# Attention's weight-value products written contiguously, eight of the 128 on VectorE

## The chip, the core and the metric

The kernel runs on one NeuronCore of a Trainium2 chip. The metric is the device time of one execution in microseconds (us). The core has five engines that run side by side: PE (TensorE, matmul; its weight loads are listed apart as PEld), DVE (VectorE), ACT (ScalarE), POOL (GpSimd) and SP, which here only issues DMAs. Each engine executes its own instructions in order and waits for other engines on semaphores. SBUF is the working memory of 128 partitions, PSUM holds what PE writes.

## What is computed

A block over 2048 tokens of width 576: the input plus a sliding, dilated attention plus a dense layer with mish, both fed with the layer-normed input.

```python
def _A_ref(x, wqkv, wo):
    H = 32; Dh = D // H                      # 18
    W, dil = 8, 2
    qkv = (x @ wqkv) split into q, k, v of 32 heads
    idx = pos[:, None] - (arange(W) * dil)[None, :]
    logits = einsum("bhsd,bhswd->bhsw", q, k[idx]) * scale   # -1e9 where idx < 0
    attn = softmax(logits)
    o = einsum("bhsw,bhswd->bhsd", attn, v[idx])
    return o @ wo
def _B_ref(x, w1, b1, w2):
    h = x @ w1 + b1                          # 4608 wide
    return (h * tanh(softplus(h))) @ w2
xn = layernorm(x)
return x + _A_ref(xn, wqkv, wo) + _B_ref(xn, w1, b1, w2)
```

Each token attends to 8 earlier tokens, two apart. The change concerns the line with `o`: 8 weights times 8 value vectors of 18 numbers, summed over the 8.

## The kernel before

The tokens are taken in two halves of 1024. Matmuls are made from fp32 numbers that are split into a rounded part and a remainder, so most operands exist twice, and ACT, DVE and POOL spend much of their time making those splits. PE runs the projections of q, k and v (L360, in the second half partly L478), the first dense layer (L706, L712) and the second dense layer (L809 in the first half, L898 in the second), then the output projection (L1028). Results of the second dense layer are added up by DVE from PSUM into SBUF: L813 in the first half, L904 in the second. They use the four PSUM banks of the tag `out`; each group of six matmuls fills one bank, and PE can write a bank again once DVE has read it. L751 on DVE adds up parts of the first dense layer from the four banks of the tag `h`.

The attention isn't done on PE. It is a generator, `attention(hf)`, one for each half, that works through 8 pairs of units, a unit being two heads (36 numbers). Token position is laid out as 128 partitions x 8 tokens (`TJ`). For each pair:

- scores: for each of the two units `k` and each half `c` of the tokens, POOL multiplies q with a window of k (L583, two instructions of 576 elements, output `pr`), and DVE sums over the 18 numbers of a head (L588);
- softmax: DVE takes maxima, sums and reciprocals (L602 to L614), ACT the exponential (L608);
- weights times values: for each unit `k` and head `h`, POOL multiplies the weights `L` with a window of v (L621, two instructions of 576 elements, output `pv`), and DVE sums over the 8 window positions into `og` (L627).

The products `pr` and `pv` share two buffers. The sum of one step (`red`) is held back by one step: `flush()` at the start of the next step issues it. The steps of the generator are spread over the program by a plan with due times, in which everything is placed at numbered positions among PE's items; the resulting order on each engine is fixed. So where an instruction stands is set by the code's order alone, and an engine that waits at one of them holds up all that stand behind it on that engine.

In L619 to L627 `pv` is laid out token, number, window position. The sum over the window then reads 8 neighbouring floats, and the multiply, which runs token, window position, number, writes with a step of 8 floats.

Of the kernel before, what the change touches and what calls it, by code (L numbers as in the profile page):

```python
# [8 lines left out]
F32 = mybir.dt.float32  # L9
F32R = mybir.dt.float32r  # L10
AF = mybir.ActivationFunctionType
ALU = mybir.AluOpType
AX = mybir.AxisListType.X

S, D, F = 2048, 576, 4608
H, DH, W, DIL = 32, 18, 8, 2
HALO = (W - 1) * DIL
P = 128
# [4 lines left out]
TJ = SH // P  # L23
# [6 lines left out]
PU = 2  # L30
# [14 lines left out]
def block_kernel(ctx: ExitStack, tc: tile.TileContext, x, wq, wo, w1, b1, w2, mask, out):  # L45
    nc = tc.nc
# [8 lines left out]
    sb = ctx.enter_context(tc.tile_pool(name="sb", bufs=2))  # L55
# [87 lines left out]
    def newton1():  # L143
        newton(rs1, ve1, y1, nc.gpsimd)
        nc.gpsimd.tensor_mul(nm1, mv1[:, :, 0:1], rs1)
        nc.gpsimd.tensor_scalar(nm1, nm1, -1.0, None, op0=ALU.mult)
# [372 lines left out]
    def load_kv(hf, i, part):  # L519
        g, u = divmod(i, UQ)  # L520
        t = odd.tile([P, TJ + HALO, CU], F32, tag="kv", bufs=4, name=f"kv{part}_{hf}_{i}")
        src = kv_d[g][part * UQ + u, hf * SH, 0:1]
        nc.sync.dma_start(
            t.rearrange("p t c -> p (t c)"),
            bass.AP(tensor=src.tensor, offset=src.offset, ap=[[TJ * CU, P], [1, (TJ + HALO) * CU]]))
        return t

    def load_kq(hf, i):
        g, u = divmod(i, UQ)
        k = load_kv(hf, i, 0)  # L530
        q = odd.tile([P, TJ, CU], F32, tag="q", bufs=2, name=f"q_{hf}_{i}")
        nc.sync.dma_start(q, q_d[g][u, hf * SH:(hf + 1) * SH, :]
                          .rearrange("(p j) c -> p j c", j=TJ))
        return k, q

    def win(kv, c0, cn, j0, jn):
        base = kv[:, j0, c0:c0 + 1]
        return bass.AP(tensor=base.tensor, offset=base.offset,
                       ap=[list(base.ap[0]), [CU, jn], [DIL * CU, W], [1, cn]])
# [10 lines left out]
    def soon(slots, phase, fn, *key):  # L550
        i = now[0] // U + slots
        if phase == 3 and i == at["m", 0, 1, 0]:
            phase = 5
        put(i * U + phase, fn, " ".join(str(x) for x in key))
# [6 lines left out]
    def attention(hf):  # L561
        kqs = [load_kq(hf, k) for k in range(PU)]
        yield
        behind = [None]

        def flush():
            if behind[0] is not None:
                behind[0]()
                behind[0] = None

        for pair in range(NQ * UQ // PU):
            n = f"{hf}_{pair}"
            vs, nxt = [], []
            L = sb.tile([P, PU, TJ, W, 2], F32, tag="L", bufs=2, name=f"L_{n}")
            hj = TJ // 2
            for k, (kt, q) in enumerate(kqs):
                for c in range(2):
                    flush()
                    pr = sb.tile([P, hj, W, CU], F32, tag="pr", bufs=2, name=f"pr_{n}_{k}_{c}")
                    j0 = c * hj  # L580
                    hh = hj // 2
                    for x in range(0, hj, hh):
                        nc.gpsimd.tensor_tensor(  # L583
                            out=pr[:, x:x + hh], in0=q[:, j0 + x:j0 + x + hh, None, :].to_broadcast([P, hh, W, CU]),
                            in1=win(kt, 0, CU, j0 + x, hh), op=ALU.mult)

                    def red(pr=pr, k=k, j0=j0, L=L):
                        nc.vector.tensor_reduce(  # L588
                            L[:, k, j0:j0 + hj].rearrange("p j w h -> p (j w h)"),
                            pr.rearrange("p j w (h d) -> p (j w h) d", h=2), axis=AX, op=ALU.add)  # L590
                    behind[0] = red
                    if k == 0:
                        vs.append(load_kv(hf, pair * PU + c, 1))
                    yield
            flush()
            if hf == 0:
                lm = L[0:2].rearrange("p k j w h -> p k (j w h)")
                nc.vector.tensor_add(lm, lm, mk[:, None, :].to_broadcast([2, PU, TJ * W * 2]))
            m = odd.tile([P, PU * TJ, 2], F32, tag="m", bufs=2, name=f"m_{n}")
            Lf = L.rearrange("p k j w h -> p (k j) w h")  # L600
            Lt = Lf.rearrange("p j w h -> p j h w")
            nc.vector.tensor_reduce(m, Lt, axis=AX, op=ALU.max)  # L602
            mb = m[:, :, None, :].to_broadcast([P, PU * TJ, W, 2])
            nc.vector.tensor_sub(Lf, Lf, mb)
            Ls = L.rearrange("p k j w h -> p (k j w h)")
            if (hf, pair) == (0, 4):
                soon(1, 0, lambda: nc.scalar.preload_act_table_set("natural_log_exp_and_others"), "exp", n)
            soon(1, 0, lambda Ls=Ls: nc.scalar.activation(Ls, Ls, AF.Exp, scale=SCALE), "exp", n)  # L608
            if (hf, pair) == (0, 4):
                soon(1, 0, root1, "exp", n)  # L610
            yield
            nc.vector.tensor_reduce(m, Lt, axis=AX, op=ALU.add)
            nc.vector.reciprocal(m, m)
            nc.vector.tensor_mul(Lf, Lf, mb)  # L614
            og = sb.tile([P, TJ, PU * CU], F32, tag="og", bufs=1, name=f"og_{n}")
            for k, vt in enumerate(vs):
                for h in range(2):
                    flush()
                    pr = sb.tile([P, TJ, DH, W], F32, tag="pr", bufs=2, name=f"pv_{n}_{k}_{h}")  # L619
                    for x in range(0, TJ, hj):  # L620
                        nc.gpsimd.tensor_tensor(  # L621
                            out=pr[:, x:x + hj].rearrange("p j d w -> p j w d"),
                            in0=L[:, k, x:x + hj, :, h:h + 1].to_broadcast([P, hj, W, DH]),
                            in1=win(vt, h * DH, DH, x, hj), op=ALU.mult)

                    def red(pr=pr, og=og, c0=k * CU + h * DH, last=(k, h) == (PU - 1, 1), pair=pair):
                        nc.vector.tensor_reduce(og[:, :, c0:c0 + DH], pr, axis=AX, op=ALU.add)  # L627
                        if last:
                            nc.sync.dma_start(
                                o_d[hf][:, pair * PU * CU:(pair + 1) * PU * CU]  # L630
                                .rearrange("(p j) c -> p j c", j=TJ), og)
                    behind[0] = red
                    if (hf, pair, k, h) == (0, *(4, 0, 1)):
                        newton1()
                    if k == 0 and (pair + 1) * PU + h < NQ * UQ:
                        nxt.append(load_kq(hf, (pair + 1) * PU + h))
                    yield
            kqs = nxt
        flush()
        yield  # L640
# [661 lines left out]
    def spot(hf, q, i):  # L1302
        return at["s", hf, q, i]
# [48 lines left out]
    for m, lists in ((0, DIFFS), (1, DIFFS), ("w", DIFFS), ("w", SPLITS)):  # L1352
        for n, steps in enumerate(lists):
            for st_ in steps.split():
                f = dict(l=d_load, s=d_sum, h=d_high, o=d_low, k=d_keep)[st_[0]]
# [43 lines left out]
    for n in range(8):  # L1399
        c, k = divmod(n, 4)  # L1400
        d = i + (0, 1, 3, 5, 7, 9, 11, 13)[n]
        before(d, lambda c=c, k=k: s_step(1, c, k))
        d = max(d + 2, (at["q", 1, 1, 1, 2], at[("z", 1, 2)])[c] if k == 3 else 0)
# [47 lines left out]
    for i in range(len(plan)):  # L1451
        w = [r_ for m, r_ in zip(marks, rate) if m <= i][-1:] or [0]
# [4 lines left out]
    k = marks[0] - 1  # L1457
    for n in range(2 * steps):
        t = n * total / (2 * steps)
        if n == steps:  # L1460
            k = max(k, spot(1, 0, 0) + 1)
        k = next(k for k in range(k + 1, len(plan)) if T[k + 1] > t and ok[k])
        hf = n // steps
        if n % steps == 0:
            before(k - 4, lambda hf=hf: (att.__setitem__(hf, attention(hf)), next(att[hf])), f"first {hf}")
        before(k, lambda hf=hf: next(att[hf], None), f"att {n}", 2)
        cuts.append(k)
# [5 lines left out]
    j = items[7 * (OC - 1) + 2][2]  # L1473
# [64 lines left out]
```

## Time and profile before

| | us |
|---|---|
| median of 3 runs | 1105.64 |
| lowest, highest | 1104.11, 1105.72 |
| the profiled execution: time | 1108.94 |
| the profiled execution: first to last instruction | 1106.8 |

The granted TensorE clock of the profiled execution is 0.997 on the mean. A row of a group names the source line, the engine, the operation, output<-inputs, the shapes and the count, then the busy time in us and the mean of one in ns, and behind the bar the idle time of the engine just before them with what ended it. A row of the timeline has the start and the length in us, then the same names; `x4` merges four neighbours, and the idle time before stands in brackets. Ends of PE's rows are modelled, so that a row may run a little into the next.

### The profile page before, as it was taken

How to read it: one execution, taken by the hardware profiler on the slowest of the kernel's cores; microseconds unless marked ns; L12 is line 12 of the kernel's file. 1: busy time of each engine (PE TensorE's matmuls, PEld its weight loads, DVE VectorE, ACT ScalarE, POOL GpSimd, SP SyncE). 2: the span in 40 equal slices, each digit the busy share in tenths (PEclk: the TensorE clock that was granted, in tenths of full speed). 3: DMA queues.
4: the chain of work that ended last, by engine and by line, in shares of the span. 5: the costliest groups of instructions: out<-in, count | busy, mean ns of one | idle time of the engine just before them, and what ended most of it. 6: DMA issues, size and time to landing. Idle time of an engine off the chain costs nothing.

```text
span 1106.8 us, 18262 instructions
## 1 busy us (share of the span) xinstructions
PE 1096.2 (99%) x6510; PEld 1009.7 (91%) x6510; DVE 862.5 (78%) x1425; ACT 516.4 (47%) x943; POOL 837.1 (76%) x675
## 2 busy tenths in 40 slices
PE   9999999999999999999999998999999999999998
PEld 8999989999999999999999887999999999999998
DVE  6447699999898888888746467788888768789876
ACT  5543646446456455546333253534444443444332
POOL 2598787897678676888799658787697978678852
PEclk9999999999999999999999998999999999999999
DMA  6789897889789698888799696665666665675863
GB/s 237 247 282 304 270 329 251 307 318 339 282 272 323 246 326 308 307 314 278 251 296 325 174 335 244 238 241 213 211 215 249 242 249 193 237 257 177 290 207 104
DMA packets 166909, 290.23 MB, mean 262 GB/s; under 512 B 31234, under 2 KB 106532, under 8 KB 166820
## 3 DMA queue, kind: packets, MB, share of 16 engines
q1 hardware_dynamic: 166820, 289.08, 75.9%
q8 instruction: 51, 0.84, 0.3%
q14 instruction: 38, 0.31, 0.1%
HBM read 170.71 MB, written 118.32 MB: 261 GB/s over the span
## 4 chain that ended last, share of the span: by engine, by line
PE 96%; DVE 1%; DMA 1%; issue 1%; ACT 0%; DVEq 0%
PE h L706 31%; PE po L809 20%; PE po L898 18%; PE pq L360 11%; PE h L712 6%; PE o L1028 5%; PE z L478 3%; DMA z_B<-kept_wq 1%; PE ta L86 0%; PE ot L942 0%; PE ot L958 0%; DMA acc<-in_x 0%; DVE st L123 0%; PE ot L960 0%; DVE accP L904 0%
## 5 line engine op out<-in xcount | busy, mean ns | idle before, releaser
L809 PEld LDWEIGHTS po<-w,act 128*128 128x128 f32 x1728 | 236.4, 188 | 6.3 <-DVE acc L813 0.4
L809 PE MATMUL po<-w,act 128*128 128x288 f32 x1728 | 240.9, 295 | 0.0
L898 PEld LDWEIGHTS po<-pw,u 128*128 128x128 f32 x1512 | 206.6, 188 | 4.7
L898 PE MATMUL po<-pw,u 128*128 128x288 f32 x1512 | 209.6, 295 | 0.0
L583 POOL TENSOR_TENSOR pr<-q,kv 128x576 f32<-128x576 f32 x128 | 192.1, 1527 | 12.3 <-DVE og L627 8.6
L621 POOL TENSOR_TENSOR pv<-L,kv 128x576 f32<-128x576 f32 x128 | 176.4, 1480 | 27.3 <-ACT rt L740 16.0
L813 DVE TENSOR_TENSOR acc<-po,acc 128x288 f32<-128x288 f32 x288 | 118.7, 448 | 32.9 <-PE po L809 31.7
L360 PE MATMUL pq<-wq,xt 128*128 128x432 f32 x672 | 136.2, 361 | 1.3 <-ACT xt L92 1.1
L904 DVE TENSOR_TENSOR accP<-po,accP 128x288 f32<-128x288 f32 x240 | 101.2, 450 | 41.2 <-PE po L898 40.2
L360 PEld LDWEIGHTS pq<-wq,xt 128*128 128x128 f32 x672 | 125.1, 188 | 8.2 <-ACT xt L92 1.7
L706 PE MATMUL h<-xt,t 128*128 128x512 f32 x432 | 111.6, 394 | 0.3 <-DVE c L751 0.3
L706 PE MATMUL h<-S,t 128*128 128x512 f32 x432 | 110.3, 391 | 0.0
L706 PE MATMUL h<-xt,wa 128*128 128x512 f32 x432 | 105.8, 394 | 2.8 <-DVE rm L751 2.8
L706 PEld LDWEIGHTS h<-xt,wa 128*128 128x128 f32 x432 | 81.7, 190 | 20.7 <-DVE rm L751 3.2
L627 DVE TENSOR_REDUCE og<-pv 128x144 f32<-128x1152 f32 x64 | 85.8, 1343 | 18.3 <-POOL pv L621 18.2
L706 PEld LDWEIGHTS h<-xt,t 128*128 128x128 f32 x432 | 80.0, 190 | 15.6 <-DVE c L751 0.6
L588 DVE TENSOR_REDUCE L<-pr 128x64 f32<-128x1152 f32 x64 | 85.6, 1342 | 7.2 <-POOL pr L583 7.1
L706 PEld LDWEIGHTS h<-S,t 128*128 128x128 f32 x432 | 78.2, 188 | 13.0
L762 POOL TENSOR_TENSOR act<-c,act 128x512 fp32r<-128x512 f32 x28 | 38.8, 1388 | 41.5 <-ACT act L757 41.2
L752 ACT ACTIVATE c<-c,b1c 128x512 f32<-128x512 f32 x54 | 39.1, 724 | 57.8 <-DVE c L751 57.7
L860 POOL TENSOR_TENSOR u<-rm,u 128x512 fp32r<-128x512 f32 x29 | 40.5, 1400 | 23.4 <-ACT u L853 23.4
L740 ACT COPY c<-h 128x512 f32<-128x512 f32 x54 | 31.5, 584 | 53.4 <-PE h L712 26.9
(269 smaller groups left out, 1927.6 us busy)
## 6 DMA issues: line engine op xcount, KB each, us to landing
kv<-kv_d SPq DMA_DIRECT2D x64, 396.0 KB, 4.6
pw<-kept_T SPq DMA_DIRECT2D x36, 576.0 KB, 4.5
kept_t<-t SPq DMA_DIRECT2D x36, 512.0 KB, 5.0
t<-kept_t SPq DMA_DIRECT2D x36, 512.0 KB, 5.3
kept_B<-w SPq DMA_DIRECT2D x54, 288.0 KB, 4.4
pw<-kept_B SPq DMA_DIRECT2D x27, 576.0 KB, 6.8
rw<-in_w SPq DMA_DIRECT2D x36, 320.0 KB, 4.4
kept_wa<-wa SPq DMA_DIRECT2D x18, 640.0 KB, 5.5
```

The costliest lines, as they stand in the source:

```text
L360: nc.tensor.matmul(pq[:, 0:432], XT[:, xi, tok], wt[wi][:, hl, 0:432], start=i == 0, stop=i == len(seq) - 1)
L583: nc.gpsimd.tensor_tensor(out=pr[:, x:x + hh], in0=q[:, j0 + x:j0 + x + hh, None, :].to_broadcast([P, hh, W, CU]), in1=win(kt, 0, CU, j0 + ...
L588: nc.vector.tensor_reduce(L[:, k, j0:j0 + hj].rearrange("p j w h -> p (j w h)"), pr.rearrange("p j w (h d) -> p (j w h) d", h=2), axis=AX, ...
L621: nc.gpsimd.tensor_tensor(out=pr[:, x:x + hj].rearrange("p j d w -> p j w d"), in0=L[:, k, x:x + hj, :, h:h + 1].to_broadcast([P, hj, W, DH]),
L627: nc.vector.tensor_reduce(og[:, :, c0:c0 + DH], pr, axis=AX, op=ALU.add)
L706: nc.tensor.matmul(ph, wt[:, wl, wk * P:(wk + 1) * P], X[:, xs, :], start=first and i == 0, stop=last and i == len(seq) - 1, skip_group_ch ...
L712: nc.tensor.matmul(ph, wt[:, wl, off * P:(off + 1) * P], X[:, xs, :], start=False, stop=wl == 1, skip_group_check=True)
L809: nc.tensor.matmul(po, acts[hf, q, b, j][:, al, tok], done["w2", hf, 2 * q + j][:, wl, c * HC:(c + 1) * HC], start=i == 0, stop=i == 5)
L813: nc.vector.tensor_tensor(out=t, in0=po, in1=t, op=ALU.add)
L898: nc.tensor.matmul(po, units[e, k, qq][:, al, tok], w[:, qq, wl, :], start=i == 0, stop=i == 5)
L904: nc.vector.tensor_tensor(out=t, in0=po, in1=t, op=ALU.add)
L1028: nc.tensor.matmul(h, l, r_, start=first and n == 0, stop=n == len(seq) - 1, skip_group_check=True)
```

## The change

`pv` is laid out token, window position, number. The multiply writes neighbouring floats, and the sum reads with a step of 18 floats. In pairs 3 and 7 of each half, the products of the last head (unit 1, head 1) are issued on DVE: two instructions in each of four places, 8 of 128.

```diff
-                    pr = sb.tile([P, TJ, DH, W], F32, tag="pr", bufs=2, name=f"pv_{n}_{k}_{h}")
+                    pr = sb.tile([P, TJ, W, DH], F32, tag="pr", bufs=2, name=f"pv_{n}_{k}_{h}")
                     for x in range(0, TJ, hj):
-                        nc.gpsimd.tensor_tensor(
-                            out=pr[:, x:x + hj].rearrange("p j d w -> p j w d"),
+                        (nc.vector if (pair % 4, k, h) == (3, PU - 1, 1) else nc.gpsimd).tensor_tensor(
+                            out=pr[:, x:x + hj],
                             in0=L[:, k, x:x + hj, :, h:h + 1].to_broadcast([P, hj, W, DH]),
                             in1=win(vt, h * DH, DH, x, hj), op=ALU.mult)
...
-                        nc.vector.tensor_reduce(og[:, :, c0:c0 + DH], pr, axis=AX, op=ALU.add)
+                        nc.vector.tensor_reduce(og[:, :, c0:c0 + DH], pr.rearrange("p j w d -> p j d w"), axis=AX, op=ALU.add)
```

Below are rows of the engines' orders: the line, the operation, output<-inputs and the shape; `x2` is two in a row. In a `pv` or `pr` name the numbers are pair, unit and head (or token half) and a running number.

On POOL, early in the first half, at a product that stays (`tt` and `t` are splits of the dense weights, `twT` sums of the second weight, `act` a split activation):

```order
 L251 TENSOR_TENSOR tt_2_1412<-rw_4_1274,tt_2_1411 128x256
 L266 TENSOR_TENSOR t_0_2_1417<-tt_2_1411,t_0_2_1417 128x512
-L621 TENSOR_TENSOR pv_0_1_1_1463<-L_0_784,kv_0_1_898 128x4x8x18 x2
+L621 TENSOR_TENSOR pv_0_1_1_1463<-L_0_784,kv_0_1_898 128x576 x2
 L314 TENSOR_TENSOR twT_1_1466<-rw_3_1188,twT_1_1466 128x288
 L762 TENSOR_TENSOR act_1_3_1487<-c_0_1_1476,act_1_3_1487 128x512
```

It stands where it stood; its output is one run of 576 instead of four dimensions. The same holds for all 120 that stay.

On POOL, in the first half at pair 3, the first of the four places:

```order
 L251 TENSOR_TENSOR tt_13_4621<-rw_27_4392,tt_13_4621 128x256
 L251 TENSOR_TENSOR tt_13_4622<-rw_26_4390,tt_13_4621 128x256
-L621 TENSOR_TENSOR pv_3_1_1_4628<-L_3_3688,kv_0_7_3740 128x4x8x18 x2
 L583 TENSOR_TENSOR pr_4_0_0_4677<-q_8_4181,kv_0_8_4179 128x576 x2
 L314 TENSOR_TENSOR twT_12_4695<-rw_24_4451 128x288
```

The pair of products is gone from POOL; the scores of the next pair follow directly. On DVE, at the same place:

```order
 L762 TENSOR_TENSOR act_1_22_4577<-c_0_11_4468,act_1_22_4577 128x512
 L627 TENSOR_REDUCE og_3_4175<-pv_3_1_0_4404 128x8x18
+L621 TENSOR_TENSOR pv_3_1_1_4628<-L_3_3688,kv_0_7_3740 128x576 x2
 L762 TENSOR_TENSOR act_0_23_4641<-mn_0_23_4639,act_0_23_4641 128x512
 L627 TENSOR_REDUCE og_3_4175<-pv_3_1_1_4628 128x8x18
```

The pair stands behind the sum of the product before it and ahead of its own sum, with what stood between them now behind the pair. On DVE, at the last of the four places, pair 7 of the second half (`u` are splits for the second dense layer, `rm` and `h` parts of the first, `accP` the sums that L904 adds into):

```order
 L860 TENSOR_TENSOR u_0_1_11438<-ra_7492,u_0_1_11438 128x512
 L627 TENSOR_REDUCE og_7_11367<-pv_7_1_0_11441 128x8x18
+L621 TENSOR_TENSOR pv_7_1_1_11493<-L_7_11077,kv_1_15_11189 128x576 x2
 L751 TENSOR_TENSOR rm_7497<-h_1_17_11348,rm_7497 128x512
 L904 TENSOR_TENSOR accP_0_7643<-po_6_0_0_11498,accP_0_7643 128x288
```

Here the pair stands ahead of an L751 and of the L904 that read PE's banks. The orders of PE, ACT and SP are the same as before.

## The prediction

> **What bounds the kernel now.** I read the page's first part, then who waits for whom on PE, then the groups by line, then the timeline at the places that the change touches.
>
> ```profile
> span 1106.8 us, 18262 instructions
> PE 1096.2 (99%) x6510; PEld 1009.7 (91%) x6510; DVE 862.5 (78%) x1425; ACT 516.4 (47%) x943; POOL 837.1 (76%) x675
> ```
>
> PE is busy for 1096.2 of 1106.8 us. All that any other engine can cost or give back is what PE stands idle, 10.6 us, and whatever PE loses because its clock fell after such a stand. The waits on PE say who ended that idle time (columns: in total, how often, the longest):
>
> ```profile
> PE h L706 <- DVE rm L751: 2.8, 1, 2.8
> PE warm L76 <- POOL ident masks.py:199: 1.3, 1, 1.3
> PE pq L360 <- ACT xt L92: 1.1, 2, 0.6
> PE h L706 <- ACT rt L740: 0.7, 1, 0.7
> PE z L478 <- ACT zkv L487: 0.6, 1, 0.6
> ```
>
> None of these names a line of the attention's weight-value products (L621 on POOL, L627 on DVE). The attention is on the side; it reaches PE only by making the in-order DVE late for something that PE needs. One wait stands out, 2.8 us on DVE at L751; I come back to it as a rival.
>
> **The change part by part.** These groups carry the prices (busy us and mean ns, then idle time before them and what ended it):
>
> ```profile
> L583 POOL TENSOR_TENSOR pr<-q,kv 128x576 f32<-128x576 f32 x128 | 192.1, 1527 | 12.3 <-DVE og L627 8.6 <-DVE L L588 3.5
> L621 POOL TENSOR_TENSOR pv<-L,kv 128x576 f32<-128x576 f32 x128 | 176.4, 1480 | 27.3 <-ACT rt L740 16.0 <-issue 3.3 <-DVE L L614 2.8
> L627 DVE TENSOR_REDUCE og<-pv 128x144 f32<-128x1152 f32 x64 | 85.8, 1343 | 18.3 <-POOL pv L621 18.2
> L588 DVE TENSOR_REDUCE L<-pr 128x64 f32<-128x1152 f32 x64 | 85.6, 1342 | 7.2 <-POOL pr L583 7.1
> L612 DVE TENSOR_REDUCE m<-L 128x32 f32<-128x256 f32 x16 | 6.6, 411 | 4.9 <-ACT L L608 4.8
> L907 POOL TENSOR_TENSOR accP<-accP,accP 128x576 f32<-128x576 f32 x12 | 17.0, 1432 | 1.8 <-DVE accP L907 1.4 <-DVE accP L904 0.3
> ```
>
> *1. POOL writes contiguously (120 products stay there).* The strided write costs nothing today: L621 with it takes 1480 ns, contiguous products of the same size take 1527 (L583) and 1432 (L907). So the bounds are 47 ns worse and 48 ns better, 120 x 0.048 = 5.8 us of POOL either way, and I take zero. Only L627 waits for L621, PE never does; POOL is idle for 1106.8 - 837.1 = 269.7 us, which covers 5.8 us. On the path: 0.
>
> *2. DVE reads with a stride (64 reduces).* The inner step becomes 18 floats, 72 bytes. No row has such a read on DVE. The nearest is L612, a reduce on the same engine whose inner step is two floats: from L612 (256 elements, 411 ns) and the contiguous L588 (1152, 1342) the slope is (1342 - 411) / 896 = 1.04 ns an element, with 411 - 256 x 1.04 = 145 ns fixed, so a step of two costs nothing that shows. The lower bound is 1343 ns as now (a read cannot be faster than the contiguous one). For the upper bound I take the slowest handling of the same tile, POOL's two products, 2 x 1480 = 2960 ns, or 1.6 us more for each reduce and 103 us of DVE over 64. I take the value of the nearest row, no change, and keep the upper end for the rivals. On the path: 0.
>
> *3. Eight products move from POOL to DVE, two at each of four places.* POOL loses 8 x 1.48 = 11.8 us. DVE gains 8 products of 576 elements with two operands in SBUF; the nearest row is L266 on the same shape (count, then min/median/max in ns):
>
> ```profile
> L266 DVE TENSOR_TENSOR w<-rw,w x21: 741/750/1971, 102.2 to 503.9; 128x576 fp32r<-128x576 f32 x21
> ```
>
> 0.75 us when alone, up to 1.97 when a POOL instruction is under way. A pair is 1.5 to 3.9 us; where POOL works beside it I take 2.0. DVE executes in order, so what stands behind the pair is late by that much. The first place, in order of time (POOL, DVE, PE):
>
> ```profile
> 378.85 2.96 POOL L621 TENSOR_TENSOR pv<-L,kv 128x576 f32<-128x576 f32 x2
> 381.95 3.26 POOL L583 TENSOR_TENSOR pr<-q,kv 128x576 f32<-128x576 f32 x2
> ...
> 380.53 1.34 DVE L627 TENSOR_REDUCE og<-pv 128x144 f32<-128x1152 f32 x1
> 382.19 1.74 DVE L762 TENSOR_TENSOR act<-mn,act 128x512 fp32r<-128x512 f32 x1 [0.32 <-ACT act L757]
> 386.96 1.22 DVE L813 TENSOR_TENSOR acc<-po,acc 128x288 f32<-128x288 f32 x3
> ...
> 385.14 3.34 PE L809 MATMUL po<-w,act 128*128 128x288 f32 x24
> 389.69 3.34 PE L809 MATMUL po<-w,act 128*128 128x288 f32 x24
> ```
>
> POOL's next product (L583 at 381.95) writes the buffer that the reduce at 380.53 empties, so it cannot start before 381.87 with the change either: nothing is gained on POOL. On DVE the pair starts at 381.80 and ends about 383.8 (at most 385.7); L762, the second reduce and the three L813 move by 383.8 - 382.2 = 1.6 us (at most 3.5). Queued behind are the L813, for which PE waits: the first ends at 386.96 + 0.46 = 387.42, its PSUM bank is written again at 389.69, slack 2.3 us. PE loses 0, at most 1.2.
>
> The second place lies in the z stage. DVE has idle time in front and behind:
>
> ```profile
> 611.60 1.35 DVE L627 TENSOR_REDUCE og<-pv 128x144 f32<-128x1152 f32 x1 [2.28 <-POOL pv L621]
> 621.77 1.35 DVE L588 TENSOR_REDUCE L<-pr 128x64 f32<-128x1152 f32 x1 [1.69 <-POOL pr L583]
> ```
>
> The 1.69 us behind it take nearly all of the 2.0. PE: 0. The third place:
>
> ```profile
> 820.88 0.69 DVE L751 TENSOR_TENSOR ra<-h,ra 128x512 f32<-128x512 f32 x1 [0.92 <-PE h L712]
> 825.41 1.75 DVE L904 TENSOR_TENSOR accP<-po,accP 128x288 f32<-128x288 f32 x4
> ...
> 828.32 3.33 PE L898 MATMUL po<-pw,u 128*128 128x288 f32 x24
> ```
>
> The idle 0.92 us take part of the 2.0, so L904 is 1.1 us late (at most 3.0); its first bank is free at 825.9 and wanted at 828.3, slack 2.4. PE: 0, at most 0.6. The fourth:
>
> ```profile
> 1014.15 1.34 DVE L627 TENSOR_REDUCE og<-pv 128x144 f32<-128x1152 f32 x1
> 1016.01 1.53 DVE L904 TENSOR_TENSOR accP<-po,accP 128x288 f32<-128x288 f32 x4
> 1020.13 0.81 DVE L904 TENSOR_TENSOR accP<-po,accP 128x288 f32<-128x288 f32 x2
> ...
> 1018.42 1.68 POOL L847 TENSOR_TENSOR rm<-rt,rm 128x512 f32<-128x512 f32 x1 [0.50 <-DVE u L860]
> ...
> 1018.61 8.62 PE L898 MATMUL po<-pw,u 128*128 128x288 f32 x64
> ```
>
> Here POOL, without its products, has nothing to do until DVE releases L847, so the pair runs alone: 1.5 us, and nothing absorbs it before 1020.13. The bank of that L904 is free at 1020.59 and wanted by the fifth group of the run of 64, at 1018.61 + 8.62 x 24 / 64 = 1021.8: slack 1.2. PE loses 0.3, at most 2.7.
>
> Sum: 0 + 0 + 0 + 0.3 = 0.3 us, with 1.2 + 0.6 + 2.7 = 4.5 at most. The profiled execution took 1108.94 us, 2.1 outside its span of 1106.8; by its own time the change makes 1109.2. It is 3.3 above the median of the runs, 1105.64, to which I carry the difference: **about 1106.0**. If the cover were gone everywhere, the four pairs would cost 4 x 2.0 = 8 us.
>
> **Rivals.** *A: the strided read runs at half the rate (slower).* If each element 72 bytes away takes two steps, a reduce is 145 + 2 x 1198 = 2541 ns, 1.2 us more, 77 us of DVE in all. DVE has room in sum (862.5 + 77 = 939 of 1106.8), so it decides where slack behind a reduce is under 1.2 us. The tightest that I found:
>
> ```profile
> 199.41 1.34 DVE L627 TENSOR_REDUCE og<-pv 128x144 f32<-128x1152 f32 x1
> 200.67 1.53 DVE L813 TENSOR_TENSOR acc<-po,acc 128x288 f32<-128x288 f32 x4
> ...
> 201.32 3.35 PE L809 MATMUL po<-w,act 128*128 128x288 f32 x24
> ```
>
> The bank is free at 201.1 and wanted at 201.32: 1.0 of the 1.2 us would reach PE. Most are looser (2.3 and 2.4 above). Reading PE's rows behind each reduce in this way I count eight places at 0.2 to 1.0, say 5 us, and the first, third and fourth place with two slow reduces each (1.6 + 2.4 - 2.3, 1.1 + 2.4 - 2.4, 1.5 + 2.4 - 1.2), some 5 us more, give 1105.6 + 10 = **1116**. Against it: L612 shows no penalty, but its step stays small.
>
> [...]
>
> *B: the long stall goes (faster).* PE's longest wait comes from here:
>
> ```profile
> 671.05 7.24 DVE L860 TENSOR_TENSOR u<-rm,u 128x512 fp32r<-128x512 f32 x1 [2.16 <-ACT u L853]
> ...
> 676.09 1.52 PE L706 MATMUL h<-xt,wa 128*128 128x512 f32 x6
> 680.40 2.93 PE L706 MATMUL h<-xt,wa 128*128 128x512 f32 x6 [2.79 <-DVE rm L751]
> ...
> 687.92 3.33 PE L898 MATMUL po<-pw,u 128*128 128x288 f32 x24
> ...
> 664.10:691.80 27.70, 24.91 (x129) 21.64 (x128) 20.07 (x24) 10.20 (x19) 22.65 (x18) 0.88 0.64 243
> ```
>
> One DVE subtraction took 7.24 us while POOL ran five instructions without a gap. PE then stood for 2.79 us, and its clock fell: the 20 matmuls from 680.40 to 687.92 took 7.5 us where six had just taken 1.52 (20 / 6 x 1.52 = 5.1), and the granted clock of that slice (the last row, a stretch of the span by engine) is 0.88. Together 2.8 + 2.4 = 5.2 us. The change alters POOL's products shortly before; if POOL's instructions fall otherwise, the stall may not come: 1105.6 - 5.2 = **1100.4**. Against it: the stage is led by PE, nothing is moved between the second and the third place, and the products' durations hardly change.
>
> *C: another such stall comes.* Each moved product has two SBUF operands as that L860, and POOL's pattern shifts; one stall more is 5.2 on top of the forecast: **1111.2**. Against it: L266 above never exceeds 1971 ns, so a wait of several POOL instructions is rare.
>
> That the change doesn't do what it says is excluded: the eight products stand on DVE in its order.
>
> **How the numbers follow.** My forecast 0.50, A 0.22, B 0.16, C 0.12. A measurement of this kernel can tell about 0.2% from no change, that is 1103.4 to 1107.9. Faster: B and 0.05 of the forecast's spread, 0.21. Slower: A, C and 0.03 of the forecast (the bound of 4.5), 0.37. Same: 0.42. The range reaches from just below B to just above A: 1099.5 to 1117.0, which leaves out part of A (its upper end is open) and a little of B.
>
> **What would show it.** Step 1: L621 on POOL stays within 50 ns of 1480. Step 2: L627 stays at 1343 ns; 2541 is A, something between pays a part of it. Step 3: L621 on DVE between 0.75 and 2.0 us, POOL idle in front of L583 at the first place where its products stood. PE's waits: L751 with 2.8 us again, or gone (B), or a second one (C). I am wrong if PE's idle time grows by several us with L813 or L904 as its releaser.

## The result, and the profile after

| | median us | lowest, highest |
|---|---|---|
| before | 1105.64 | 1104.11, 1105.72 |
| changed | 1115.01 | 1114.73, 1115.99 |

The ratio is 1.0091, with a 95% interval of 1.0068 to 1.0114: slower by about 9.4 us. Beside the experiments below the kernel before ran 57 more times, 43 of them from 1102.0 to 1105.4 us at a granted clock of 0.999 to 1.0 and 14 from 1106.6 to 1110.3 us, 13 of these at 0.997 to 0.999; its profiled execution, 1108.94 us at 0.997, is of the longer kind. The profiled execution of the changed kernel took 1115.99 us. The top of its page, and the groups that answer to those of before:

```profile
span 1113.9 us, 18258 instructions
PE 1097.3 (99%) x6510; PEld 1007.2 (90%) x6510; DVE 914.8 (82%) x1433; ACT 516.5 (46%) x943; POOL 823.9 (74%) x667
...
L583 POOL TENSOR_TENSOR pr<-q,kv 128x576 f32<-128x576 f32 x128 | 193.9, 1540 | 29.5 <-DVE og L627 26.3
L621 POOL TENSOR_TENSOR pv<-L,kv 128x576 f32<-128x576 f32 x120 | 153.1, 1300 | 31.4 <-ACT rt L740 15.8
L627 DVE TENSOR_REDUCE og<-pv 128x144 f32<-128x1152 f32 x64 | 143.0, 2237 | 13.1 <-POOL pv L621 12.9
L588 DVE TENSOR_REDUCE L<-pr 128x64 f32<-128x1152 f32 x64 | 85.7, 1342 | 7.0 <-POOL pr L583 7.0
```

The reduce L627 went from 1343 to 2237 ns, 0.89 us more, 64 times: 57 us of DVE. L588, the same count of neighbouring floats, stayed at 1342. POOL's products became shorter, 1300 for 1480 ns. POOL now waits for L627 where it did so little before (26.3 us in front of L583, 8.6 before), because the two buffers come free later.

What this does to PE is seen in the list of what PE waited for in the changed kernel (us in total, how often, the longest):

```profile
PE po L898 <- DVE accP L904: 3.1, 3, 1.3
PE po L809 <- DVE acc L813: 1.8, 2, 1.3
PE pq L360 <- ACT xt L92: 1.4, 2, 0.7
PE warm L76 <- POOL ident masks.py:199: 1.3, 1, 1.3
PE h L706 <- DVE rt L751: 1.0, 1, 1.0
```

The two accumulations that empty PE's `out` banks head the list; in the trace of before they were not in it. The weight loads (PEld) show it more fully. The first two rows are from before, the last two from the changed kernel; the number behind the second bar is the idle time ahead of the group's loads:

```profile
L809 PEld LDWEIGHTS po<-w,act 128*128 128x128 f32 x1728 | 236.4, 188 | 6.3 <-DVE acc L813 0.4
...
L898 PEld LDWEIGHTS po<-pw,u 128*128 128x128 f32 x1512 | 206.6, 188 | 4.7
```

```profile
L809 PEld LDWEIGHTS po<-w,act 128*128 128x128 f32 x1728 | 236.4, 188 | 10.1 <-DVE acc L813 3.5
...
L898 PEld LDWEIGHTS po<-pw,u 128*128 128x128 f32 x1512 | 206.4, 188 | 11.9 <-DVE accP L904 4.8
```

Ahead of the second layer's matmuls the loads stood for 6.3 + 4.7 = 11.0 us before and 10.1 + 11.9 = 22.0 us after. One of the places, the tight one that the prediction showed at 199.41, in the timeline of the changed kernel:

```profile
200.17 2.17 DVE L627 TENSOR_REDUCE og<-pv 128x144 f32<-128x1152 f32 x1
202.27 1.53 DVE L813 TENSOR_TENSOR acc<-po,acc 128x288 f32<-128x288 f32 x4
...
202.76 3.46 PE L809 MATMUL po<-w,act 128*128 128x288 f32 x24 [1.35 <-DVE acc L813]
```

L813 now begins at 202.27 instead of 200.67, its first bank is free at 202.7, and PE, which wanted it 1.35 us earlier, starts right then. One reduce adds only 0.89 us; this one itself began 0.76 us later than before (200.17 for 199.41), for DVE had not stood idle since the reduce before it, at 182.69, and carried that one's delay along. So DVE's lateness adds up from one reduce to the next.

### The profile page after: what moved, and what is told of

It is laid out like the page before. It is cut to its first block, busy times and chain, and to the rows that moved or that the text cites. A ratio compares the mean times of both kernels' runs of the same rounds, so it can differ in the third digit from the quotient of the medians.

```text
span 1113.9 us, 18258 instructions
## 1 busy us (share of the span) xinstructions
PE 1097.3 (99%) x6510; PEld 1007.2 (90%) x6510; DVE 914.8 (82%) x1433; ACT 516.5 (46%) x943; POOL 823.9 (74%) x667
## 4 chain that ended last, share of the span: by engine, by line
PE 79%; DVE 11%; DMA 4%; POOL 3%; issue 1%; ACT 1%; SPq 1%; DVEq 0%; POOLq 0%; ACTq 0%
PE h L706 23%; PE po L809 17%; PE po L898 14%; PE pq L360 11%; PE o L1028 5%; DVE og L627 4%; PE h L712 4%; PE z L478 3%; DMA pw<-kept_T 1%; POOL pr L583 1%; DVE accP L904 1%; POOL act L762 1%; DMA z_B<-kept_wq 1%; DVE u L860 1%; DMA t<-kept_t 1%
## 5 line engine op out<-in xcount | busy, mean ns | idle before, releaser
L809 PEld LDWEIGHTS po<-w,act 128*128 128x128 f32 x1728 | 236.4, 188 | 10.1 <-DVE acc L813 3.5
L898 PEld LDWEIGHTS po<-pw,u 128*128 128x128 f32 x1512 | 206.4, 188 | 11.9 <-DVE accP L904 4.8
L583 POOL TENSOR_TENSOR pr<-q,kv 128x576 f32<-128x576 f32 x128 | 193.9, 1540 | 29.5 <-DVE og L627 26.3
L621 POOL TENSOR_TENSOR pv<-L,kv 128x576 f32<-128x576 f32 x120 | 153.1, 1300 | 31.4 <-ACT rt L740 15.8
L627 DVE TENSOR_REDUCE og<-pv 128x144 f32<-128x1152 f32 x64 | 143.0, 2237 | 13.1 <-POOL pv L621 12.9
L813 DVE TENSOR_TENSOR acc<-po,acc 128x288 f32<-128x288 f32 x288 | 115.9, 446 | 20.7 <-PE po L809 20.1
L904 DVE TENSOR_TENSOR accP<-po,accP 128x288 f32<-128x288 f32 x240 | 100.0, 450 | 30.0 <-PE po L898 28.5
L706 PE MATMUL h<-xt,t 128*128 128x512 f32 x432 | 110.7, 391 | 1.1 <-DVE rt L751 1.0
L706 PE MATMUL h<-S,t 128*128 128x512 f32 x432 | 110.4, 391 | 1.0 <-DMA t<-kept_t 1.0
L706 PE MATMUL h<-xt,wa 128*128 128x512 f32 x432 | 104.2, 390 | 0.0
L706 PEld LDWEIGHTS h<-xt,wa 128*128 128x128 f32 x432 | 81.0, 188 | 17.3
L706 PEld LDWEIGHTS h<-xt,t 128*128 128x128 f32 x432 | 79.0, 188 | 16.7 <-DVE rt L751 1.5
L588 DVE TENSOR_REDUCE L<-pr 128x64 f32<-128x1152 f32 x64 | 85.7, 1342 | 7.0 <-POOL pr L583 7.0
L706 PEld LDWEIGHTS h<-S,t 128*128 128x128 f32 x432 | 78.0, 188 | 14.2 <-ACT rm L752 1.4
L752 ACT ACTIVATE c<-c,b1c 128x512 f32<-128x512 f32 x54 | 39.1, 724 | 66.7 <-DVE c L751 66.5
L706 PE MATMUL h<-S,wc 128*128 128x512 f32 x216 | 55.8, 393 | 0.7 <-ACT rt L740 0.7
L860 POOL TENSOR_TENSOR u<-rm,u 128x512 fp32r<-128x512 f32 x29 | 40.7, 1407 | 17.5 <-ACT u L853 17.5
```

What stands on the lines that cost most here:

```text
L583: nc.gpsimd.tensor_tensor(out=pr[:, x:x + hh], in0=q[:, j0 + x:j0 + x + hh, None, :].to_broadcast([P, hh, W, CU]), in1=win(kt, 0, CU, j0 + ...
L588: nc.vector.tensor_reduce(L[:, k, j0:j0 + hj].rearrange("p j w h -> p (j w h)"), pr.rearrange("p j w (h d) -> p (j w h) d", h=2), axis=AX, ...
L621: (nc.vector if (pair % 4, k, h) == (3, PU - 1, 1) else nc.gpsimd).tensor_tensor(out=pr[:, x:x + hj], in0=L[:, k, x:x + hj, :, h:h + 1].to ...
L627: nc.vector.tensor_reduce(og[:, :, c0:c0 + DH], pr.rearrange("p j w d -> p j d w"), axis=AX, op=ALU.add)
L706: nc.tensor.matmul(ph, wt[:, wl, wk * P:(wk + 1) * P], X[:, xs, :], start=first and i == 0, stop=last and i == len(seq) - 1, skip_group_ch ...
L809: nc.tensor.matmul(po, acts[hf, q, b, j][:, al, tok], done["w2", hf, 2 * q + j][:, wl, c * HC:(c + 1) * HC], start=i == 0, stop=i == 5)
```

## The experiments

The experiments ran on three chips, e1 to e5 on the first, e6 to e9 on the second, e10 to e13 on the third, each beside the kernel before on the same chip. e3, e7, e8, e11 and e12 sum the wrong numbers; only their times and traces are used. Theory 1: the read with a step of 18 floats lengthens each reduce by 0.89 us, DVE is then late with L813 and L904, and that is the loss. Theory 2: the eight moved products make a good part of it. Theory 3: they give part of it back.

| run | what | median us | before | ratio (95%) |
|---|---|---|---|---|
| e1 | layout alone | 1112.29 | 1103.02 | 1.0082 (1.0065 to 1.0098) |
| e2 | move alone, old layout | 1106.33 | 1103.02 | 1.0034 (1.0019 to 1.0048) |
| e3 | the change, neighbours read | 1102.96 | 1103.02 | 1.0002 (0.9992 to 1.0011) |
| e5 | before, longer reduce | 1117.09 | 1103.02 | 1.0127 (1.0112 to 1.0142) |
| e6 | the change again | 1116.56 | 1103.61 | 1.0111 (1.0086 to 1.0137) |
| e7 | stepped read alone | 1115.29 | 1103.61 | 1.0109 (1.0076 to 1.0142) |
| e8 | contiguous write alone | 1102.41 | 1103.61 | 0.9985 (0.9973 to 0.9997) |
| e10 | a layout in pairs | 1102.58 | 1104.88 | 0.997 (0.9954 to 0.9986) |
| e11 | write alone + six tokens | 1116.16 | 1104.88 | 1.0092 (1.0064 to 1.012) |
| e12 | write alone + five tokens | 1112.96 | 1104.88 | 1.0066 (1.0043 to 1.0088) |
| e13 | layout alone, again | 1110.91 | 1104.88 | 1.0059 (1.0041 to 1.0076) |

The kernel before spread over 1102.0 to 1110.3 us on the third chip (12 of its 26 times lie above 1106), over 1102.5 to 1108.6 on the second (2 of 13 above 1106) and over 1102.3 to 1105.4 on the first. So the ratios on the third chip are pulled down, and across chips I compare the medians of the variants rather than their ratios; that takes the chips to be alike, which the shortest times of before (1102.3, 1102.5 and 1102.0) support.

**Which part costs: e1, e2, e3.** e1 takes the choice of engine out of the change, e2 puts it into the kernel before, e3 lets the changed kernel's reduce read neighbours:

```diff
 e1
-(nc.vector if (pair % 4, k, h) == (3, PU - 1, 1) else nc.gpsimd).tensor_tensor(
+nc.gpsimd.tensor_tensor(
 e3
-nc.vector.tensor_reduce(og[:, :, c0:c0 + DH], pr.rearrange("p j w d -> p j d w"), axis=AX, op=ALU.add)
+nc.vector.tensor_reduce(og[:, :, c0:c0 + DH], pr.rearrange("p j w d -> p j (w d)").rearrange("p j (d w) -> p j d w", w=W), axis=AX, op=ALU.add)
```

> The new layout, all 128 products on POOL. Theory 1 (the stepped read makes each of the 64 reduces 0.89 us longer, and that is the whole loss): 1114 to 1116 us, L627 at 2240 ns. Theory 2 (the eight moved products carry a good part of the loss, as each stands in front of PE's accumulations): 1106 to 1111 us. Theory 3 (the moved products give part of the loss back): 1117 us or more.

> The old layout (POOL and DVE write with a step, the reduce reads neighbours), the eight products on DVE. Theory 1: 1105 to 1107 us, as the move alone was priced at 0.3 us. Theory 2: 1109 us or more. L621 on DVE between 0.75 and 1.0 us when alone if a stepped write costs DVE nothing, 1.2 us or more if a step costs it in writing as in reading.

> The changed kernel, but the reduce reads eight neighbouring floats of the new layout, so that it sums the wrong numbers; nothing else differs. Theory 1: the loss is gone, 1104 to 1107 us, L627 back at 1343 ns. Theory 2: 1109 us or more.

e3 is the decisive one: with nothing changed but the step of the read, the loss of the whole change is gone, 1102.96 against 1103.02 us. Its trace has L627 back at its old time, and the idle time ahead of the second layer's weight loads back at 6.2 + 5.0 = 11.2 us:

```profile
L627 DVE TENSOR_REDUCE og<-pv 128x144 f32<-128x1152 f32 x64 | 85.9, 1343 | 16.7 <-POOL pv L621 16.6
...
L809 PEld LDWEIGHTS po<-w,act 128*128 128x128 f32 x1728 | 236.5, 188 | 6.2 <-DVE acc L813 0.4
L898 PEld LDWEIGHTS po<-pw,u 128*128 128x128 f32 x1512 | 206.8, 188 | 5.0 <-DVE accP L904 0.3
```

The profiled spans of the two kernels that differ only in the read are 1100.5 and 1113.9 us, 13.4 us apart. 10.8 of that is the growth from 11.2 to 22.0 us ahead of these loads, and 2.7 the same ahead of two groups of the first layer's loads (L706).

e1 has 9.3 us without any moved product. Its 1112.29 us lie below the band that I had given; the kernel before took 2.6 us less on this chip than in the result above. Theories 2 and 3 fall as the main cause. e2 took 3.3 us more than before, where the move had been priced at 0.3. Its group of moved products, and that of the changed kernel, which writes contiguously, from the views of the line L621:

```profile
L621 DVE TENSOR_TENSOR pv<-L,kv x8: 1268/1304/2484, 382.0 to 1012.7; 128x576 f32<-128x576 f32 x8
```

```profile
L621 DVE TENSOR_TENSOR pv<-L,kv x8: 739/754/1986, 384.7 to 1022.2; 128x576 f32<-128x576 f32 x8
```

At the minimum a product takes DVE 1268 ns when it writes with a step of 8 floats and 739 ns when it writes neighbours: a stepped write costs DVE as well, and more than the 0.2 us that it costs POOL.

**Is it only the time on DVE: e5, e11, e12.** e5 leaves the kernel before as it is and has DVE sum six of the eight tokens once more ahead of each reduce; e11 and e12 do so with six and five tokens on the new layout, with neighbours read:

```diff
+nc.vector.tensor_reduce(og[:, 0:6, c0:c0 + DH], pr[:, 0:6], axis=AX, op=ALU.add)
 nc.vector.tensor_reduce(og[:, :, c0:c0 + DH], pr, axis=AX, op=ALU.add)
```

> The kernel before with no layout change and no move; in front of each of the 64 reduces DVE sums six of the eight tokens once more (864 neighbouring elements, about 1.04 us, 0.96 us from start to start), which the reduce then overwrites. Theory 1 (only the longer time on DVE counts, not how memory is read): 1114 to 1118 us. If the stepped read hurts in another way too (POOL or PE slowed by it): below 1111 us.

> The new layout, all products on POOL, the reduce reads neighbours (wrong sums), and in front of each reduce DVE sums six tokens once more (0.96 us from start to start). Differs from the longer reduce on the kernel before only in POOL's contiguous write. If the time on DVE alone counts: 1.0127 as there. If POOL's faster write takes part of the wait away: 1.0095 to 1.0115.

> The same with five tokens, 0.81 us from start to start, 0.08 us below what the stepped read adds. If only the length on DVE matters, just below the layout alone on the same chip: 1.006 to 1.008. If the stepped read has another effect beside its length: at least 0.003 away from the layout alone.

> The layout alone on the same chip as the two runs before: 1.008 as the first time.

No stepped read, and the loss is there. What five tokens take is seen in the groups of e12 (its file has one line more, so that L628 is the real reduce):

```profile
L628 DVE TENSOR_REDUCE og<-pv 128x144 f32<-128x1152 f32 x64 | 86.6, 1353 | 2.2
...
L627 DVE TENSOR_REDUCE og<-pv 128x90 f32<-128x720 f32 x64 | 57.1, 893 | 11.5 <-POOL pv L621 11.4
```

The second instruction starts when the first has ended (2.2 us of idle time stand ahead of the 64 second ones), so that the two do not overlap as I had assumed: 57.1 + 86.6 = 143.7 us, nearly what L627 takes with the step, 143.0. So e12 has the same DVE time as e13 on the same chip without a stepped read, and the ratios agree, 1.0066 and 1.0059 with overlapping intervals; the medians are 2 us apart. Six tokens add 1.04 instead of 0.89 us and cost 1116 to 1117 us. The length of the reduce is enough; the stepped read has no second effect that these runs can tell, that is none above some 2 us. e11's ratio of 1.0092 lies below both of its bands, and e13's 1.0059 below the 1.008 of e1. In both the longer times of before on that chip have a part: beside the median of its 14 times under 1106, 1103.0 us, they are 1.0119 and 1.0072. By the medians e11 is 0.9 us below e5 and e13 1.4 us below e1.

**Does POOL's faster write matter: e7, e8.** e7 is the kernel before with the stepped read alone, e8 the new layout with neighbours read and all products on POOL.

> The kernel before (POOL writes with a step, all 128 products on POOL), only the reduce reads with the step of 18 floats; on that layout it sums the wrong numbers. L627 at 2240 ns. If POOL's faster contiguous writes (1.19 instead of 1.39 us) give something back in the change: clearly slower than the layout alone, ratio 1.011 to 1.013, like the run with the longer reduce. If POOL's time counts for nothing, as the prediction had it: 1.007 to 1.0095, as the layout alone.

> The new layout with all 128 products on POOL, and the reduce reads eight neighbouring floats, so that it sums the wrong numbers: the contiguous write alone. If POOL's 0.2 us per product count for nothing: ratio 0.999 to 1.001. If they are worth something by themselves: 0.998 or less.

e8 came out between its two bands: 0.9985, by its interval at least 0.3 and at most 3 us. e7 points the same way more loosely: 1115.29 against 1112.29 and 1110.91 us with the contiguous write, but its four times reach from 1112.08 to 1118.29, and its interval overlaps that of e1. That POOL's shorter products give some 1 to 3 us back is likely, not settled.

**The change beside its parts: e6.**

> The changed kernel on the chip of the next two runs, so that it can be set beside them. If the eight moved products cost nothing: within 2 us of the run with the layout alone when both are taken relative to their kernel before, so 1.008 to 1.010. If they cost: 1.011 or more. If they give part of the loss back: 1.007 or less.

The ratio is 1.0111, at the edge of the band for "they cost", and its interval overlaps that of e1. The medians of the changed kernel, 1115.0 and 1116.6 us, stand against 1112.3 and 1110.9 us of the layout alone: on top of slow reduces the moved products cost some 3 to 6 us, though no two of these runs are from one chip. The traces bear out a part of it: PE waits 3.1 us for L904 in both traces of the changed kernel and 0.7 us in both of the layout alone (e1, e13). Without slow reduces, e3 against e8, it is 1102.96 against 1102.41. The timeline of the third place in the changed kernel shows why:

```profile
820.15 2.22 DVE L627 TENSOR_REDUCE og<-pv 128x144 f32<-128x1152 f32 x1
822.30 2.65 DVE L621 TENSOR_TENSOR pv<-L,kv 128x576 f32<-128x576 f32 x2
824.87 0.68 DVE L751 TENSOR_TENSOR ra<-h,ra 128x512 f32<-128x512 f32 x1
828.42 2.19 DVE L627 TENSOR_REDUCE og<-pv 128x144 f32<-128x1152 f32 x1
830.51 1.55 DVE L904 TENSOR_TENSOR accP<-po,accP 128x288 f32<-128x288 f32 x4
...
831.02 3.47 PE L898 MATMUL po<-pw,u 128*128 128x288 f32 x24 [1.27 <-DVE accP L904]
```

Two slow reduces and the pair in between stand ahead of one L904: it starts at 830.51 for 825.41 before, while PE's group that needs its bank was due at 829.8. The two slow reduces alone still fit: in e1, which has them without the pair, PE starts the same group without a wait.

```profile
828.84 1.54 DVE L904 TENSOR_TENSOR accP<-po,accP 128x288 f32<-128x288 f32 x4
...
829.94 3.33 PE L898 MATMUL po<-pw,u 128*128 128x288 f32 x24
```

At the fourth place it is the same: the first row is from the changed kernel, the second from e1.

```profile
1028.75 1.46 PE L898 MATMUL po<-pw,u 128*128 128x288 f32 x9 [1.31 <-DVE accP L904]
...
1025.77 4.49 PE L898 MATMUL po<-pw,u 128*128 128x288 f32 x32 [0.21 <-DVE accP L904]
```

**What a step costs by itself: e9.** Not the block; single instructions repeated three times, one engine at a time, with the step in the name (in one execution). `read` are DVE's sums, `dw` and `gw` products on DVE and POOL that write with the step, and `gb` products on POOL with one operand repeated over 18 elements.

> Not the block: one engine at a time repeats single instructions (the output is not the block's). DVE sums eights of 1152 elements read with steps of 1, 2, 3, 4, 6, 8, 9, 18 and 36 floats; DVE and then POOL multiply 576 elements and write with steps of 1, 2, 4, 8 and 16 floats. [...]

```profile
L34 DVE TENSOR_REDUCE read_eight<-src 128x144 f32<-128x1152 f32 x3 | 6.6, 2213 | 0.0
...
L34 DVE TENSOR_REDUCE read_four<-src 128x144 f32<-128x1152 f32 x3 | 6.6, 2187 | 0.0
L34 DVE TENSOR_REDUCE read_eighteen<-src 128x144 f32<-128x1152 f32 x3 | 6.3, 2095 | 0.0
L34 DVE TENSOR_REDUCE read_thirtysix<-src 128x144 f32<-128x1152 f32 x3 | 6.3, 2095 | 0.0
L34 DVE TENSOR_REDUCE read_three<-src 128x144 f32<-128x1152 f32 x3 | 5.0, 1679 | 0.0
...
L50 POOL TENSOR_TENSOR gw_eight<-a,b 128x576 f32<-128x576 f32 x3 | 4.2, 1403 | 0.0
L50 POOL TENSOR_TENSOR gw_one<-a,b 128x576 f32<-128x576 f32 x3 | 4.2, 1397 | 0.1
L34 DVE TENSOR_REDUCE read_one<-src 128x144 f32<-128x1152 f32 x3 | 4.0, 1347 | 5.0 <-DMA src<-in_x 5.0
L34 DVE TENSOR_REDUCE read_two<-src 128x144 f32<-128x1152 f32 x3 | 4.0, 1344 | 0.0
L50 POOL TENSOR_TENSOR gb_eight<-a,b 128x576 f32<-128x576 f32 x3 | 3.7, 1228 | 0.2
L50 DVE TENSOR_TENSOR dw_eight<-a,b 128x576 f32<-128x576 f32 x3 | 3.6, 1203 | 0.0
L50 DVE TENSOR_TENSOR dw_four<-a,b 128x576 f32<-128x576 f32 x3 | 3.6, 1194 | 0.0
L50 POOL TENSOR_TENSOR gb_one<-a,b 128x576 f32<-128x576 f32 x3 | 3.5, 1166 | 0.0
...
L50 DVE TENSOR_TENSOR dw_two<-a,b 128x576 f32<-128x576 f32 x3 | 2.3, 766 | 0.0
L50 DVE TENSOR_TENSOR dw_one<-a,b 128x576 f32<-128x576 f32 x3 | 2.3, 763 | 0.0
```

DVE reads with a step of two floats as fast as neighbours (1344 and 1347 ns); a step of three is in between (1679), and from four to 36 all lie between 2.1 and 2.2 us (2187 at four, 2213 at eight, 2095 at 18 and 36), so that a step longer than four adds next to nothing. DVE's writes rise between two and four as well (763 at a step of one, 766 at two, 1194 at four). POOL's plain product shows no such rise (1397 at a step of one, 1403 at eight); with one operand repeated over 18 elements, as the weights in L621, it gains 62 ns by writing neighbours. The 0.2 us that L621 gained in the kernel is more than that, and where the rest comes from is open.

**A layout that avoids both: e10.** A step of two cost DVE's reduce nothing in e9 (1344 ns), so pairs of numbers can be kept together: POOL writes runs of two floats, and the reduce reads with a step of two.

```diff
-pr = sb.tile([P, TJ, DH, W], F32, tag="pr", bufs=2, name=f"pv_{n}_{k}_{h}")
+pr = sb.tile([P, DH // 2, TJ, W, 2], F32, tag="pr", bufs=2, name=f"pv_{n}_{k}_{h}")
-out=pr[:, x:x + hj].rearrange("p j d w -> p j w d"),
+out=pr[:, :, x:x + hj].rearrange("p e j w r -> p j w e r"),
...
-nc.vector.tensor_reduce(og[:, :, c0:c0 + DH], pr, axis=AX, op=ALU.add)
+nc.vector.tensor_reduce(og[:, :, c0:c0 + DH].rearrange("p j (e r) -> p e j r", r=2),
+                        pr.rearrange("p e j w r -> p e j r w"), axis=AX, op=ALU.add)
```

> A third layout of the products, all 128 on POOL: POOL writes runs of two floats, and the reduce reads with a step of two floats, which cost nothing where single instructions were repeated. L627 at 1343 ns; L621 between 1.19 us (as contiguous) and 1.39 us (as before). If POOL keeps the gain of the contiguous write, 0.9985 of before as the write alone; if runs of two cost POOL as single floats do, 1.000.

```profile
L621 POOL TENSOR_TENSOR pv<-L,kv 128x576 f32<-128x576 f32 x128 | 162.9, 1298 | 28.2 <-DMA t<-kept_t 16.0 <-DVE L L614 3.5 <-issue 2.9
L627 DVE TENSOR_REDUCE og<-pv 128x144 f32<-128x1152 f32 x64 | 85.8, 1343 | 16.4 <-POOL pv L621 16.2
```

POOL has its 1298 ns and DVE keeps its 1343, so the loss of the changed kernel is avoided. By its ratio of 0.997 (0.9954 to 0.9986) it is also a little faster than the kernel before, but that rests on the longer times of before: its 12 times lie between 1101.84 and 1103.73, about where the better half of the times of before lies on this chip (1102.01 to 1104.33). The longer times didn't come in e10; why they didn't is open, and beside the shorter ones no gain can be told.

## Why the prediction was right, and where it was wrong

The measured 1115.0 us lies in the range, at the time worked out for rival A (1116, chance 0.22), and its direction, slower, had 0.37 against 0.42 for the same. The likeliest forecast, 1106.0, was wrong, and the sign that I had named for being wrong came: PE's idle time grew by several us with L813 and L904 as its releasers.

- **What bounds the kernel**: right. PE stayed at 99% before and after, and the loss came on the path that the prediction gave for anything that makes DVE late: PE waiting for L813 and L904, and a smaller part for the first layer's banks (L751).
- **Step 1, POOL's contiguous write**: the size was wrong, 180 ns less per product (1480 to 1300) where the bounds were 47 worse and 48 better. L583 and L907, the rows that I took, have no operand that is repeated over neighbouring elements, and e9 shows POOL at 1166 with such an operand and at 1397 without, so they were no measure for L621. That PE sees almost nothing of it held: e8 is 0.9985.
- **Step 2, the stepped read: this step failed.** I took "the value of the nearest row, no change", from L612, whose step is two floats. The runs show 2237 ns for 1343, and e9 shows that a step of two is no measure for one of 18 (1344 and 2095 ns). The prediction had noted that L612's step stays small; I still let it carry the central value, though this was an open cost that counted 64 times and stood ahead of PE's accumulations. The lower bound held: none of the nine steps of e9 took less than 1344 ns.
- **Step 3, the moved products**: about right in its own terms. Alone a product takes 754 ns in the median (L266: 750), 1986 at most (1971). With neighbours read, the moves cost nothing that can be told (e3). The slack reading held only with the old reduces; with the slow ones, cover ran out at the third place and at the fourth, 1.27 and 1.31 us of waiting.
- **Rival A**: the way to PE was right, through reduces that are slower and a DVE that is late with L813 and L904; the price of a reduce was too high, 1.2 us instead of 0.89. No run shows the two steps an element that A's sum is made of: with the same fixed 145 ns an element takes 1.82 ns instead of 1.04, which is not a doubling. The 5 us at tight places were too low: the layout alone costs 9.3 us on the first chip, for I took each place by itself, while DVE's lateness adds up, as at 199.41. The 5 us at the moved pairs agree with the 3 to 6 us measured. That the sum came within 1 us of the result is partly luck: the two errors went against each other.
- **Rival B**: the 7.24 us subtraction and PE's stall behind it are not in the changed kernel's trace. The prediction made its sum against a profiled execution 3.3 us above the median and carried only the difference over. That the stall of 5.2 us belonged to that execution and not to the three runs fits, as do the clocks of the longer times of before, but no second trace of before was taken, so this is argued and not shown. What such a stop costs is seen a second time, in the trace of e12 (its L752 is L751 of the other kernels):

```profile
786.48 6.05 PE L899 MATMUL po<-pw,u 128*128 128x288 f32 x24 [3.04 <-DVE rt L752]
```

PE stood for 3.04 us, the granted clock was 0.83 from 780 to 800 us, and the 24 matmuls took 6.05 us instead of 3.33. This execution took 1117.86 us, the other six of e12 1111.05 to 1114.06.
- **Rival C**: such waits do come. The changed kernel has one, and the layout alone (twice), the stepped read alone and the change again have one at the same instruction, of 5.5 to 5.9 us; the contiguous write alone has one of 4.28 us at another place:

```profile
884.98 5.51 DVE L860 TENSOR_TENSOR u<-ra,u 128x512 fp32r<-128x512 f32 x1
```

PE didn't wait there in any of the five; the price of 5.2 us that I gave to any of them was that of one place.

## What to carry to other kernels

When a layout change swaps the side that steps, price the step on the engine that has the least room: POOL's products bore it for about 0.2 us each (1480 against 1300 ns), two to a reduce, and on an engine with room; DVE's reduce paid 0.89 us. If no row of the profile shows the access, the nearest row is no price; multiply the open cost by its count and look at the slack behind it before taking zero. And where DVE sums fp32 as here, keep two neighbouring floats together (1344 ns at a step of two floats, 1679 at three, 2187 at four): a layout in pairs let one engine write short runs and the other read with a step of two, with POOL at the time of its contiguous write (1298 ns) and DVE at that of its contiguous read (1343 ns).

## What the runs showed of the hardware that was not expected

- A read with a step from 4 to 36 floats costs DVE's reduce about 0.75 to 0.87 us over 1152 elements when alone, by which the element goes from 1.04 ns to between 1.7 and 1.8 ns, and not to twice its time; a step of three costs 0.33 us (e9). In the kernel the step of 18 took 0.14 us more than alone (2237 and 2095 ns).
- DVE pays for stepped writes as well: 576 products took 1203 ns at a step of eight and 763 contiguous (e9), 1268 against 739 in the kernel (e2 and the change).
- POOL's product with one operand repeated along the run is faster than with two plain ones, 1166 and 1397 ns (e9).
- A DVE instruction with two operands in SBUF that takes 0.68 us alone (L860) can take as long as several POOL instructions in a row: 7.24 us in the trace of before, while POOL ran five without a gap, and 5.51 in the changed one. All other such instructions in these two traces stayed below 2.1 us. What decides between the two is open.
- After PE had stood for 2.79 us (before) and 3.04 us (e12), the granted clock was 0.88 over the 28 us and 0.83 over the 20 us around it; in the changed kernel, with no stand above 1.35 us, it was 1.0 on the mean.
